# Two key/value heads per load on alternate partitions, in a decode kernel of two attention and two MLP layers

## The chip, the core and the metric

The kernel runs on one core of one Trainium2 chip. The metric is the device time of one execution in microseconds; the kernel before took 231.98 us, the median of three runs (231.31 to 232.46). A core has five engines with queues of their own: TensorE (PE in the profile, with PEld for its weight loads), VectorE (DVE), ScalarE (ACT), GpSimd (POOL) and SyncE (SP), which here issues nearly all DMAs. Each engine works through its own list in order and waits on semaphores for the others.

## The reference

Eight sequences, one new token each, width D = 448. One layer is attention over a cached window and then an MLP; the pair is applied twice with the same weights and the same cache:

```python
x = x + attention(layernorm(x), k_cache, v_cache, wq, wo)   # 16 query heads, 8 key/value heads, Dh 256
x = x + mlp(layernorm(x), w1, w2)                           # 448 -> 1792 -> 448, silu
x = x + attention(layernorm(x), k_cache, v_cache, wq, wo)
x = x + mlp(layernorm(x), w1, w2)
```

Only the last 1024 of the 4096 cached positions count. For each sequence and each of its 8 key/value heads that is 1024 x 256 bf16 of K and as much of V: 512 KB each, 128 such pieces, 67.1 MB in all, beside some 10 MB of weights. Two query heads share one key/value head. Each piece is needed in both layers and is loaded once.

## The kernel before

**Loads.** `load_kv` fetches one head of K or V (512 KB) into one of R = 30 buffers `slot`, by one DMA (L496): partition p holds positions 8p to 8p+7, a row of 4 KB. The order is K heads 0 to 7 of sequence 0, V heads 0 to 7, K of sequence 1, and so on (`seq`, `pump`). Load n waits until load n-30 has been used for the last time. `wq` (rows of 8 KB, contiguous) is loaded first, `w2` and `wo` behind K of sequence 0, `w1` behind V of sequence 0.

**One sequence b.** K is turned in place by VectorE in 32 x 32 blocks of 4 bytes (`transposes`, L639): four heads with one instruction of 128x1024, four with two of 128x512. `scores` (L656) multiplies the 16 query heads with K: 32 matmuls of 256 columns for each half of the heads (four heads side by side on four column groups of TensorE), read with a step of two elements. `softmax` takes the maximum (L673), spreads it over the partitions with a float32 matmul against `quad` (L675, L677), the exponential (L688), a reordering matmul against `perm` (L690, 256 columns) and a turn (L692) that gives the weights of the values. `products` (L703) multiplies them with V: four matmuls of 512 columns for each head, each writing rows that the next head overwrites from row 4(8-kvh) down. In layer 1 the last two heads (`late`, `products_late`, L712) go to an own bank, so that the other six heads can be evicted (L725), turned (L729, L733) and multiplied with `wo` (L754) before the last V has landed. `fold` and `xcols` (L760, L529, L532, L765) bring the residual row into columns; `chain` is the MLP (L544, L549, L798, L806, L818) and the query projection of layer 2 (L833, L838, L839, L846, L850). Then layer 2 scores, softmax and products on the same K and V follow, after which their slots are free.

**Order.** Layer 2 of sequence b is mixed with layer 1 of sequence b+1. The order of every engine is written out as lists of task numbers (`ORDER`); semaphores are derived from it. `warm` puts groups of four matmuls without use (L781) into TensorE's list.

**End.** The MLP of layer 2 is done for sequences 0 to 6 together (`final_rows`; its constants L874, L878, L880) and for sequence 7 alone (`final_last`: L798, L801, L803, L959, L963).

Of the kernel before, what the change touches and what calls it, by code (L numbers as in the profile page):

```python
# [14 lines left out]
        "196 69 74 86 87 88 89 197 198 92 136 94 199 137 138 139 148 149 161 150 200 151 201 154 202 203 157 204 205 "  # L15
        "159 206 207 208 209 228 229 211 213 225 226 231 227 233 235 214 237 215 240 216 242 217 218 248 249 219 275 "
        "276 251 257 220 254 259 264 262 325 277 279 280 278 281 282 221 312 222 313 267 314 315 287 288 223 318 289 "
        "321 290 224 326 327 328 329 323 330 331 343 297 344 333 300 340 341 351 342 346 335 352 353 302 348 354 355 "
        "350 356 357 371 374 376 336 358 409 382 383 368 410 411 385 388 393 391 398 396 412 413 414 415 416 446 447 "
        "448 449 401 337 338 421 452 422 423 424 459 455 339 431 460 461 462 463 434 457 464 465 484 476 477 467 436 "  # L20
        "469 473 474 479 475 481 485 486 483 487 504 509 507 488 489 490 491 515 516 501 542 543 518 521 524 526 531 "
        "529 544 470 546 547 548 549 545 534 579 554 580 581 582 555 556 557 471 585 564 472 588 592 567 593 594 595 "
        "596 590 617 618 597 598 569 609 619 610 600 606 607 612 608 620 621 614 616 602 637 640 642 622 623 675 624 "
        "676 648 649 634 603 604 651 654 657 659 664 662 677 725 679 680 681 682 678 712 713 667 714 715 687 688 689 "
        "718 605 690 721 697 726 727 728 729 730 723 731 742 700 733 743 750 751 752 753 735 739 740 745 741 754 702 "
        "747 755 749 756 757 770 773 775 808 736 767 781 782 809 810 784 787 792 790 797 795 812 813 814 815 811 800 "
        "845 846 847 848 820 821 737 822 851 738 823 854 830 856 859 860 861 833 862 875 863 864 883 876 866 858 884 "
        "885 886 872 887 878 873 874 880 888 882 835 889 903 890 906 908 868 900 941 914 915 942 917 869 920 925 923 "
        "930 928 943 944 945 946 947 948 978 979 980 981 933 870 984 871 953 954 987 955 956 992 993 994 995 989 996 "
        "997 1008 991 963 999 1001 1009 966 1005 1006 1011 1007 1013 1016 1017 1002 1015 968 1018 1036 1041 1039 "  # L30
        "1019 1020 1021 1022 1023 1047 1048 1033 1074 1075 1050 1076 1053 1056 1058 1063 1061 1077 1078 1079 1066 "
        "1080 1081 1084 1085 1086 1087 1105 1106 1107 1108 1090 1111 1118 1093 1003 1004 1114 1142 1143 1144 1119 "
        "1116 1120 1121 1122 1123 1124 1145 1134 1146 1147 1126 1095 1135 1131 1132 1137 1133 1139 1148 1128 1149 "
        "1141 1129 1154 1157 1151 1159 1197 1198 1165 1166 1199 1200 1168 1130 1171 1176 1174 1181 1179 1196 1202 "
        "1250 1224 1184 1225 1226 1227 1237 1238 1239 1240 1211 1208 1233 1251 1246 1252 1253 1235 1254 1259 1248 "
        "1260 1261 1262 1256 1213 1264 1258 1266 1218 1268 1219 1271 1274 1284 1276 1221 1285 1286",
    "dve":
        "37 28 39 43 34 26 36 46 42 25 38 24 5 13 4 54 7 32 44 40 18 30 33 6 22 27 45 50 11 57 31 29 9 49 52 70 15 "
        "19 72 51 73 132 75 58 134 3 84 80 81 59 76 60 141 82 48 135 77 133 10 53 83 140 143 35 16 55 146 144 142 78 "
        "20 17 145 90 91 85 93 14 174 12 21 175 56 147 169 184 185 152 41 170 155 162 163 179 158 160 47 8 189 180 "  # L40
        "190 271 272 236 273 241 243 245 23 247 274 252 309 258 304 310 260 261 311 307 308 306 305 265 266 316 319 "
        "322 295 324 298 301 405 406 407 370 408 375 303 377 379 381 438 441 439 386 442 444 394 392 395 445 443 440 "
        "399 400 450 453 429 456 432 435 458 538 539 503 540 510 508 514 437 512 541 573 571 519 575 576 525 527 528 "
        "574 532 577 572 533 578 583 562 586 565 589 568 591 671 672 570 673 636 674 641 643 645 647 705 706 708 652 "
        "707 711 658 660 661 704 710 709 665 666 716 719 695 722 698 724 701 804 805 703 806 769 807 774 776 778 780 "
        "837 839 838 785 840 842 793 791 794 843 844 798 799 841 849 852 828 855 831 857 834 937 938 939 902 836 940 "
        "907 909 911 913 971 970 973 918 975 977 926 924 927 972 974 976 931 932 982 985 988 961 990 964 967 1070 "
        "1071 1035 1072 1042 1040 969 1046 1044 1073 1098 1100 1051 1099 1101 1057 1059 1060 1097 1064 1065 1103 "
        "1102 1104 1088 1109 1091 1112 1094 1115 1117 1096 1186 1153 1158 1188 1160 1189 1162 1187 1193 1164 1169 "
        "1190 1191 1177 1192 1194 1175 1195 1178 1182 1183 1204 1206 1228 1229 1207 1230 1231 1241 1242 1243 1244 "  # L50
        "1234 1247 1236 1209 1249 1212 1214 1215 1217 1269 1275 1277 1279 1280 1282 1283 1222 1287",
    "act":
        "2 71 164 165 166 167 171 172 176 153 177 168 178 181 182 156 183 186 187 191 188 192 210 212 230 193 232 "
        "234 238 95 173 244 246 250 253 255 263 268 317 320 296 332 299 334 345 347 349 372 378 380 367 384 369 387 "
        "389 397 402 451 454 430 433 466 468 478 480 482 505 513 511 500 517 520 502 522 530 535 584 563 587 566 599 "
        "611 601 613 615 638 644 646 633 650 635 653 655 663 668 717 720 696 699 732 744 734 746 748 771 766 777 779 "
        "783 786 788 768 796 801 850 853 829 832 865 877 867 879 881 904 899 910 912 916 901 919 921 929 934 983 986 "
        "962 998 965 1000 1010 1012 1014 1037 1045 1043 1032 1049 1034 1054 1052 1062 1067 1089 1110 1092 1113 1125 "
        "1127 1136 1138 1140 1150 1155 1152 1161 1163 1167 1201 1170 1172 1180 1203 1205 1185 1232 1245 1255 1263 "
        "1257 1265 1216 1267 1220 1272 1270 1278 1281",  # L60
    "pool":
        "0 1 79 130 131 239 269 270 256 404 403 373 390 536 506 523 537 669 639 656 670 802 772 789 803 905 935 936 "
        "922 1068 1069 1038 1055 1156 1173 1210 1273",
}

# [158 lines left out]
def bass_interleave_layers__sliding_block_cached__dense_activation_silu__decode_kernel(  # L224
# [15 lines left out]
    FC = F // P  # L240
    SCALE = float(DH) ** -0.5
    EPS = 1e-5
    R = 30
    WIDE = (0, 1, 2, 3)
    LATE = 2
    WARM = (8, 12, 5, 4, 4, 4, 4, 4, 3)
# [243 lines left out]
    def slot_key(s):  # L490
        return [("slot", s, 0), ("slot", s, 1)]
# [607 lines left out]
```

## Time and profile before

| | |
|---|---|
| median of three runs | 231.98 us (231.31 to 232.46) |
| the profiled execution's own time | 230.15 us |
| its span (first to last instruction) | 228.4 us |
| instructions | 8452, of which 3779 matmuls |
| busy: PE, PEld, DVE, ACT, POOL | 173.0, 94.1, 157.2, 71.4, 22.8 us |
| granted TensorE clock | 1.0 throughout |
| moved by DMA | 78.21 MB |

The page gives shares over the whole span. It also cuts the span into 40 slices of 5.7 us; a digit is the busy share in tenths. Groups of instructions are named by engine, line and the tiles that they write and read, with the count, the busy time together, the mean of one in nanoseconds, and what ended the idle time before them. The view by windows gives the same for any stretches one names; its last two columns are the busy share of the DMA engines and the GB/s that they moved. Where this text says when one load landed, it is the time of its issue plus its time from issue to landing in the trace. Matmul durations overlap, since matmuls are pipelined: the pace of a burst is its length divided by its count.

### The profile page before, as it was taken

To read this page: it belongs to the slowest core of one execution; us is meant where nothing else is said; L and a number is where in the kernel's file an instruction comes from. 1 tells how busy PE (TensorE), PEld (TensorE's weight loads), DVE (VectorE), ACT (ScalarE), POOL (GpSimd) and SP (SyncE) were. 2 spreads that over 40 slices of the span, in tenths; PEclk is the share of its full clock that TensorE was granted. 3 is DMA by queue.
4 is the path that set the end of the run, shared out by engine and by line. 5 is a ranking of instruction groups with operands and counts; after the bars stand their busy time and mean duration, and the time that the engine had idled before them with its cause. 6 is when DMAs were issued, how large, how long until landed. Compare 5 with 4: busy or idle time off the path is not lost.

```text
span 228.4 us, 8452 instructions
## 1 busy us (share of the span) xinstructions
PE 173.0 (76%) x3779; PEld 94.1 (41%) x3779; DVE 157.2 (69%) x369; ACT 71.4 (31%) x218; POOL 22.8 (10%) x41
## 2 busy tenths in 40 slices
PE   0020737357878989999898987888989999999894
PEld 0010623123444455445444644554445445544662
DVE  6238989878792797389459837974895589314644
ACT  2000080633302341432324142414332431353341
POOL 1000130000200210101010101110120200000020
PEclk9999999999999999999999999999999999999999
DMA  6999999999999999999999999999999999700000
GB/s 175 413 406 407 382 380 395 411 414 417 405 400 369 377 408 403 396 408 407 406 406 408 402 378 411 408 392 395 410 409 385 380 408 406 307 3 3 0 6 1
DMA packets 22681, 78.21 MB, mean 342 GB/s; under 512 B 2279, under 2 KB 5302, under 8 KB 22262
## 3 DMA queue, kind: packets, MB, share of 16 engines
q1 hardware_dynamic: 22486, 77.32, 86.6%
q8 instruction: 29, 0.48, 0.9%
q10 hardware_dynamic: 160, 0.36, 0.6%
q14 instruction: 6, 0.05, 0.1%
HBM read 77.67 MB, written 0.01 MB: 340 GB/s over the span
## 4 chain that ended last, share of the span: by engine, by line
PE 46%; DVE 31%; DMA 10%; ACT 6%; issue 4%; SPq 2%; DVEq 0%; ACTq 0%
DVE slot L639 12%; DMA slot<-in_A_k_cache_dram 10%; PE bank L656 10%; PE bank L703 7%; DVE slot L472 7%; PE pair L754 6%; PE bank L781 2%; PE pair L833 2%; ACT ot L760 2%; PE bank L675 2%; PE bank L846 2%; PE bank L712 2%; PE bank L833 2%; PE pair L529 2%; PE pair L818 1%
## 5 line engine op out<-in xcount | busy, mean ns | idle before, releaser
L639 DVE STREAM_TRANSPOSE slot<-slot 128x512 uint32<-128x512 uint32 (+1 forms) x96 | 80.2, 866 | 7.0 <-DMA slot<-in_A_k_cache_dram 6.8
L656 PE MATMUL bank<-slot,qbd 128*16 128x256 bf16 (+1 forms) x1024 | 40.9, 285 | 5.1 <-DVE slot L639 2.0
L703 PE MATMUL bank<-slot,qbd 128*24 128x512 bf16 (+6 forms) x416 | 31.1, 393 | 3.5 <-DVE qbd L692 3.3
L656 PEld LDWEIGHTS bank<-slot,qbd 128*16 128x16 bf16 (+1 forms) x1024 | 23.2, 87 | 16.7 <-ACT qbd L850 4.0
L781 PE MATMUL bank<-wq_sb,cols 128*1 128x512 bf16 x192 | 19.6, 416 | 13.9 <-DMA wq_sb<-in_A_wq_dram 13.9
L776 POOL TENSOR_TENSOR fcols<-fcols 128x1 f32<-128x1 f32 x17 | 9.4, 554 | 106.4 <-ACT fcols L774 94.5
L754 PE MATMUL pair<-wo_sb,q1s 128*1 128x449 bf16 x288 | 17.2, 353 | 1.1 <-DVE wo_sb L475 0.8
L850 ACT ACTIVATE qbd<-bank 128x256 bf16<-128x256 f32 x16 | 6.1, 384 | 33.5 <-PE bank L846 33.5
L725 ACT ACTIVATE ot<-bank,q1s 128x512 bf16<-128x512 f32 (+1 forms) x16 | 10.8, 673 | 16.4 <-PE bank L703 11.1
L626 POOL TENSOR_TENSOR qbd<-q1s,fcols 128x256 bf16<-128x256 bf16 x16 | 9.7, 614 | 59.7 <-PE bank L712 42.4
L703 PEld LDWEIGHTS bank<-slot,qbd 128*24 128x24 bf16 (+6 forms) x416 | 9.7, 92 | 11.1 <-DVE qbd L692 4.2
L692 DVE STREAM_TRANSPOSE qbd<-bank 128x256 bf16<-128x256 bf16 x17 | 8.0, 473 | 8.2 <-PE bank L690 7.9
L673 DVE TENSOR_REDUCE q1s<-bank 128x1 f32<-128x256 f32 x15 | 6.3, 423 | 8.1 <-PE bank L656 8.0
L472 DVE TENSOR_REDUCE slot<-wo_sb 128x6 f32<-128x2688 bf16 x4 | 11.8, 2948 | 0.1
L781 PEld LDWEIGHTS bank<-wq_sb,cols 128*1 128x1 bf16 x192 | 4.2, 82 | 15.4 <-issue 13.9
L674 ACT ACTIVATE q1s<-fcols,q1s 128x4 f32<-128x4 f32 x15 | 4.4, 296 | 18.7 <-DVE q1s L673 18.7
L675 PE MATMUL bank<-q1s,quad 128*128 128x4 f32 x30 | 6.0, 269 | 4.7 <-ACT q1s L674 4.5
L598 PE MATMUL pair<-slot,wq_sb 128*128 128x16 bf16 x128 | 3.6, 174 | 7.5 <-DVE slot L591 7.5
L833 PE MATMUL pair<-wq_sb,q1s 128*1 128x256 bf16 x256 | 8.9, 275 | 0.3 <-DVE q1s L765 0.3
L688 ACT ACTIVATE qbd<-bank,q1s 128x256 bf16<-128x256 f32 x15 | 7.1, 472 | 6.3 <-DVE q1s L677 6.0
L712 PE MATMUL bank<-slot,qbd 128*7 128x256 bf16 (+7 forms) x192 | 8.6, 283 | 0.6 <-DVE qbd L692 0.6
L833 PE MATMUL bank<-wq_sb,q1s 128*1 128x512 bf16 x128 | 8.8, 390 | 0.0
(168 smaller groups left out, 244.6 us busy)
## 6 DMA issues: line engine op xcount, KB each, us to landing
slot<-in_A_k_cache_dram SPq DMA_DIRECT2D x64, 512.0 KB, 8.3
slot<-in_A_v_cache_dram SPq DMA_DIRECT2D x64, 512.0 KB, 10.1
wo_sb<-in_A_wo_dram SPq DMA_DIRECT2D x4, 896.0 KB, 14.6
wq_sb<-in_A_wq_dram SPq DMA_DIRECT2D x3, 1024.0 KB, 8.0
w_sb<-in_B_w_dram SPq DMA_DIRECT2D x1, 1568.0 KB, 19.8
w_sb<-in_B_w_dram SPq DMA_DIRECT2D x1, 1344.0 KB, 17.2
wq_sb<-in_A_wq_dram ACTq DMA_DIRECT2D x1, 256.0 KB, 3.5
wq_sb<-in_A_wq_dram SPq DMA_DIRECT2D x1, 256.0 KB, 4.1
```

Source lines behind the costliest of these rows:

```text
L472: dve(lambda e, rows=rows, s=s: e.tensor_reduce(s, rows[:, :, R0:M1].rearrange("p c (a n) -> p c a n", a=2), AX.X, ALU.add, negate=True), ...
L626: pool(lambda e, k2=k2: e.tensor_tensor(qdata(0, k2), q1s[:, b, 64 * k2:64 * k2 + 64].rearrange("p (n r) -> p n r", r=2).unsqueeze(3) .bro ...
L639: dve(lambda e, v=v: e.transpose(v, v), keys, keys, 0.15 + n / 2 / 950, b, ("KW%d" if n > 1024 else "KT%d") % k)
L656: fns.append(lambda e, w=w, j=j, kv=kv, cb=cb, par=par: e.matmul(sc[32 * j:32 * j + up_to, 0:256], w, kv, start=(cb == 0 and par == 0), st ...
L675: pe(lambda e: e.matmul(mx, quad[:], mq, start=True, stop=True, skip_group_check=True), [K[4], "quad"], bk(LB[n]), 0.2, b, "mx%d" % L)
L703: pe([lambda e, t=t: e.matmul(bank[ob][32 * t:32 * t + m, :], pT_sb[L][:, 64 * t:64 * t + m], v[:, 512 * t:512 * t + 512], start=True, sto ...
L712: pe([lambda e, t=t, a=a: e.matmul(o[32 * t:32 * t + m, :], pT_sb[n][:, 64 * t + a:64 * t + a + m], v[:, 512 * t + DH * a:512 * t + DH * a ...
L725: act(lambda e: e.activation(o_t, src[1], ACTF.Copy, scale=sm[b][:, 4 * L + 3:4 * L + 4]), bk(src[0]) + [("sm", b, L, 3)], okey, 0.62, b, ...
L754: fns.append(lambda e, i=i, w=w, c0=c0: e.matmul(bank[XB][32 * (i % 4):32 * (i % 4) + 1, c0:c0 + D + 1], oT[:, oT_col(i):oT_col(i) + 1], w ...
L776: pool(lambda e: e.tensor_tensor(rhalf, var4, nhalf, ALU.pow), ["var4", "nhalf"], ["rhalf"], 0.54, b, "pow" + name)
L781: pe([lambda e, i=i: e.matmul(bank[OB[0]][32 * i:32 * i + 1, :], zero_b, wq_sb[:, 512 * i:512 * i + 512], start=True, stop=True, tile_posi ...
L833: pe([lambda e, j=j, c=c, qh=qh, k2=k2, h=h, n=n: e.matmul(qh[32 * j:32 * j + 1, :], xbt[b][:, xcol(c, k2):xcol(c, k2) + 1], view(wq_sb[:] ...
```

## The change

- One DMA loads two heads (1 MB) into a slot of 8 KB per partition; there are 15 slots. Partition 2i holds positions 16i to 16i+15 of the first head, partition 2i+1 those of the second. The two heads lie 2 MiB apart in memory. The very last load is split into two of 512 KB with rows of 4 KB.
- `transposes` does the same number and sizes of instructions. Behind the turn the two heads alternate, so `scores` reads with a step of four elements instead of two.
- `softmax`: the maximum is spread by four small float32 matmuls on column groups instead of one of 128 partitions; the reordering is four matmuls of 128 columns that write every second column, instead of one of 256.
- `products` runs per pair, in two halves (8 of the 16 positions each) that accumulate; weights that belong to the other head are zeros. The count of matmuls is the same. `late` is the last pair.
- A slot is free when both its heads are done.
- The last MLP loses one VectorE step in each half (L801); the factor moves into the last instruction, which adds the residual that ScalarE has copied out earlier. Ten small VectorE instructions of `final_rows` move to an earlier sequence (`fold_consts`).
- All lists in `ORDER` are new.

```diff
-    R = 30
-    WIDE = (0, 1, 2, 3)
+    R = 15
+    NP = HKV // 2
+    WIDE = (0, 1)
+    SLOT = 4096
...
-        dma(lambda e: e.dma_start(slots[s][:, :].rearrange("p (u d) -> p u d", d=DH),
-                                  cache[b, kvh, S0:SK, :].rearrange("(p u) d -> p u d", p=P)),
-            slot_key(s) + extra, W * DH * 2, "slot%d" % s)
+        a = cache[b, 2 * j, S0:SK, :]
+        step = SLOT // 2 if apart else SLOT
+        for h in range(SLOT // step):
+            src = bass.AP(a.tensor, a.offset + h * step, [[SLOT, 64], [SK * DH, 2], [1, step]])
...
-                    kv = slots[slot_of[b, "k", 4 * k2 + j]][:, :].rearrange(
-                        "p (u cb jj par) -> p cb par u jj", u=8, cb=4, par=2)[:, cb, par, :, :]
+                    kv = view(slots[slot_of[b, "k", 2 * k2 + j // 2]][:, :], 64 * cb + 2 * (j % 2) + par, [(256, 16), (4, 16)])
...
-            pe(lambda e: e.matmul(mx, quad[:], mq, start=True, stop=True, skip_group_check=True), [K[4], "quad"],
-               bk(LB[n]), 0.2, b, "mx%d" % L)
+            pe([lambda e, t=t: e.matmul(mx[32 * t:32 * t + 32, :], quad[:], mq[:, 4 * t:4 * t + 4], start=True, stop=True,
+                                        tile_position=(0, 32 * t), skip_group_check=True) for t in range(4)],
+               ["mq", "quad"], bk(LB[n]), 0.06, b, "mx%d" % L)
...
-        pe(lambda e: e.matmul(px, perm[:], e_sb[m], start=True, stop=True),
+        pe([lambda e, h=h, u=u: e.matmul(px[:, h:256:2], perm[h][:, 16 - 16 * u:144 - 16 * u],
+                                         e_sb[m][:, 128 * u:128 * u + 128], start=(u == 0), stop=(u == 1),
+                                         skip_group_check=True) for h in range(2) for u in range(2)],
...
-        m = 4 * (HKV - kvh)
-        pe([lambda e, t=t: e.matmul(bank[ob][32 * t:32 * t + m, :], pT_sb[L][:, 64 * t:64 * t + m],
-                                    v[:, 512 * t:512 * t + 512], start=True, stop=True, tile_position=(0, 32 * t),
-                                    skip_group_check=True) for t in range(4)],
+        m = 8 * (NP - j)
+        for h in range(2):
+            pe([lambda e, t=t, h=h: e.matmul(
+                bank[ob][32 * t:32 * t + m, :], pT_sb[L][:, 64 * t + 32 * h:64 * t + 32 * h + m],
+                v[:, 2048 * h + 512 * t:2048 * h + 512 * t + 512], start=(h == 0), stop=(h == 1),
+                tile_position=(0, 32 * t), skip_group_check=True) for t in range(4)],
...
-                dve(lambda e, t=t: e.tensor_scalar(t, t, 1.0, rhalf, op0=ALU.add, op1=ALU.mult), [("th", h), "rhalf"],
-                    [("th", h)], 0.12, b, "th" + n)
...
-        dve(lambda e: e.tensor_copy(orow, ob[:, 0:T]), bk(OB[1]) + KEY, ["orowL"], 0.18, b, "orowL")
+        dve(lambda e: e.scalar_tensor_tensor(out=orow, in0=ob[:, 0:T], scalar=rhalf, in1=res, op0=ALU.mult, op1=ALU.add),
+            bk(OB[1]) + ["rhalf", "resL"] + KEY, ["orowL"], 0.2, b, "orowL")
...
-    cap = [R - 2]
+    cap = [R - 1]
```

The new lists move these places, by the order of the instructions (counted before and after): in the last batch TensorE's list has the turn of the first six heads (L729, 12 columns) ahead of the last late products (L712, 3 rows) before, and behind all 16 late products and four other products after. VectorE's list has, at the start, three row sums of `wo` and two of `w2` ahead of the first turn of softmax (L692) before, and two and one after. At the end VectorE's copy of the seven other rows (L927) stands behind both products of the last MLP (L803) before, and between its two halves after.

## The prediction

> **What bounds the kernel now.** I read the page's slices first, to see which resource is full and until when; then windows, for the rate of loads with rows of 8 KB and of 4 KB; then, sequence by sequence, when V landed and when TensorE used it, to see which of the two waits; last the tail.
>
> ```profile
> DMA  6999999999999999999999999999999999700000
> GB/s 175 413 406 407 382 380 395 411 414 417 405 400 369 377 408 403 396 408 407 406 406 408 402 378 411 408 392 395 410 409 385 380 408 406 307 3 3 0 6 1
> ```
>
> The DMA engines are full from slice 2 to 35, until about 199 us; the remaining 29 us are a chain of small steps. So the time is the stream's length plus a tail, as long as compute keeps up with the stream.
>
> ```profile
> 8.00:12.00 4.00, 0.00 (x0) 0.00 (x0) 0.00 (x0) 0.00 (x0) 0.00 (x0) 1.00 1.01 422
> 28.00:36.00 8.00, 4.07 (x76) 1.95 (x68) 7.01 (x13) 4.69 (x14) 2.44 (x3) 1.00 1.06 381
> ...
> 60.00:64.00 4.00, 3.41 (x81) 1.76 (x79) 2.89 (x7) 1.00 (x3) 0.55 (x1) 1.00 1.03 410
> ...
> 192.00:196.00 4.00, 3.43 (x91) 2.51 (x88) 2.74 (x7) 1.15 (x4) 0.00 (x0) 1.00 1.03 411
> ```
>
> The last column of the windows is GB/s. From 8 to 12 us only `wq` moves, in rows of 8 KB: 422. From 28 to 36 us it is `w2` and `wo` in rows of 1792 B: 381. In windows of K and V alone, in rows of 4 KB, it is 410 to 412 (mean of five: 411).
>
> Now the compute. The last V head of sequences 1 to 7 landed at 73.16, 95.02, 116.00, 137.14, 157.64, 178.70 and 200.36 us; TensorE began its late products of that head (L712, 3 rows) at 74.48, 95.42, 116.45, 137.54, 158.68, 179.44 and 200.68.
>
> ```profile
> 200.41 0.26 PE L729 MATMUL bank<-sel_o,ot 128*128 128x12 bf16 x4
> 200.59 0.24 PE L694 MATMUL bank<-q1s,lsel 128*32 128x1 f32 x8
> 200.68 0.40 PE L712 MATMUL bank<-slot,qbd 128*3 128x256 bf16 x8
> 200.94 0.93 PE L754 MATMUL pair<-wo_sb,q1s 128*1 128x449 bf16 x16
> ```
>
> So compute follows the stream by 0.3 to 1.3 us. Stream and compute are balanced: a shorter stream pays only as far as the new order makes compute shorter too. TensorE is busy 17.8 of each 20 us from 80 to 180 us (mean of five windows), which at 21.03 us a sequence (126.20 us from 74.48 to 200.68, by six) is 18.7, with 2.3 us left, some of it filled with L781, which nobody needs.
>
> **The change part by part.**
>
> *Loads.* K and V are 67.1 MB: 163.3 us at 411 GB/s, 159.0 at 422, so **-4.3 us**. From the extremes (412 to 421, the second from 6 to 12 us) it is -3.5. No row of the trace shows a load that alternates between two regions 2 MiB apart; as a loss that is a rival below. I take -4.0. The dips in the GB/s row (369, 378, 380) are stalls that rows of 8 KB meet as well. At the end two loads of 512 KB with 4 KB rows cost nothing beyond before.
>
> *Freeing slots.* Load n+30 heads waits for the same score or product groups as before, two heads at a time, so at most one head's 1.28 us later. Before, the tightest issues (66.93, 72.30, 151.62, 172.60 us) landed 4.7 to 4.8 us later with the queue still full ahead of them; the last two landings are 1.25 us apart, so it never ran dry. Cost 0, and up to +1.0 if an issue comes 1.28 us later in the first two sequences, where the margin is smallest.
>
> *K by pairs.* The first head of a pair is there 1.28 us later. VectorE waits for K 6.8 us in all (9 times), only on the first heads; the last transposition of sequence 7 began at 193.16, 3.6 us after the last K landed (189.55), because it stood behind L838. So the later heads don't notice: 0, at most +1.0 where VectorE has no gap left.
>
> *Scores with a step of four.* The count and shape stay. L656 with a step of two elements runs 80 in 2.60 us, 32.5 ns each for 256 columns; L703, contiguous, 24 in 1.48 us, 61.7 ns for 512. So a step of 4 bytes costs 5% at most. A far step does cost: L884 reads 42 columns 256 bytes apart in 237 ns, L532 42 columns side by side in 182, 1.3 ns a column. The bounds for a step of 8 bytes are therefore 0 and 1.3 ns a column; nearest is L656's own 4 bytes, so I take 0. The Trainium skill (SBUF — State Buffer, "Door 1: The DMA port swizzle") says that SBUF has lines of 16 bytes, of which two accesses in a row are needed for full speed. By it a step of 8 bytes is just free and L884's is not, with which the rows agree; by it the sum stays as it is.
>
> *Reordering in softmax.* One matmul of 256 columns (283 ns) becomes four of 128 that write every second float32. Contiguous, from L738 (6 columns, 179 ns) and L690 (256, 283 ns) the slope is 0.42 ns a column, so four take about 0.23 + 3 x 0.056 = 0.40 us. L846 writes every fourth column, 64 columns at a pace of 66 ns (four begin at 64.63, 64.70, 64.76, 64.82), some 1 ns a column: four of 128 would then take 0.7. So +0.1 to +0.4 per softmax. The four small matmuls for the maximum replace L675 (0.39 us for its two passes) and resemble L694 (x8 in 0.24): -0.15. In the steady part this is spread among TensorE's gaps; in the tail only the reordering counts. I take **+0.2**.
>
> *Products.* 32 groups of the same size, nothing.
>
> *Start.* Two of the row sums before the first turn (2.95 and 1.99 us) now stand behind it. `wo` could begin at 53.34 when its sums were done (idle <- DVE L475); with one sum of `w2` less ahead it is ready about 2 us earlier, and then V's landing at 48.7 rules: products 2.1, L725 0.7, L729 0.3, L733 0.2 put it at about 52.1. This 1.2 us only lets compute catch up with the stream: 0 in the sum.
>
> *Last batch.* The turn of six heads now stands behind the late products. Before, `wo` began 0.58 us after the last landing and its 32 rows were done after 2.5 us. Now it is landing +0.3, products until +1.0 (the groups follow at 0.2 us), turn, L733 0.2, so `wo` from +1.25, done at +3.15: **+0.6**.
>
> *End.* L801 goes from both halves (0.21 and its gap: 0.26), but the copy of the seven rows (L927, 605 ns) now stands between the halves, and the second half is late by about what the first gains; of the ten constants only two memsets lay near the path. 0, within 0.2 either way.
>
> Sum: -4.0 + 0.2 + 0.6 = **-3.2 us** on the profiled execution's 230.15, which is 226.95. That execution was 1.83 us below the median of the three runs; I forecast the median: 231.98 - 3.2 = **228.8 us**. A measurement of this kernel can tell about 0.5% (1.16 us) from no change. The forecast's own range is 227.6 to 230.2: from -4.3 with no loss in the last batch to -1.8 with one of the +1.0 terms; chance 0.52.
>
> **The rivals.**
>
> *The compute keeps its pace (0.17).* The late products of the last but one head (L712, 7 rows) went from 73.85 to 199.63, 20.96 us a sequence, while the stream allowed 21.24 (71.66 to 199.10), and lagged where the stream was quick: from 137.54 to 158.68 it took 21.14 us though V came after 20.50. For it: that lag, and TensorE at 89%. Against it: sequences 4 and 6 took 20.3 us between those products (116.02 to 136.30, 157.82 to 178.06), so 20.5 is within reach. Then only the start's 1.2 us is won, the order at the end costs nothing, softmax 0.2: 231.0 us.
>
> *More is won (0.17).* The whole 4.3 is passed on, TensorE comes to the turn early enough that the last batch loses nothing, the end gains 0.2 and softmax costs its lower 0.1: 231.98 - 4.4 = 227.6 us, down to 226.4 with a start that also shortens the stream's first waits.
>
> *Slower: scores pay for the step (0.08).* The place is L656's 128 matmuls per sequence. It decides from 2.3 us / 128 = 18 ns a matmul on, TensorE's idle time. At twice the pace (+32.5 ns) it is 4.2 us a sequence, 1.9 beyond the idle time in seven sequences, and 64 matmuls in the tail, 2.1: +15 us, 247; at 1.3 ns a column far more. Against it: L656 against L703.
>
> *Slower: two regions 2 MiB apart load slower than one (0.06).* As slow as the slowest stream seen, 381 GB/s, it is 176.1 us for K and V, +12.8: 245 us; it decides from 411 GB/s down. For it there is no row, against it only that `wq` at 422 shows what 8 KB rows can do in one region. The Trainium skill (DMA: Bandwidth & Descriptors, "Latency and other measured facts") gives 164 GB/s for rows 2 MiB apart against 207 at 512 KiB or 214 with padding. By that ratio, 0.77, K and V would take 212 us and the kernel 281; but there every row was 2 MiB from the last, here neighbours are 8 KB apart within each head, so it speaks for the direction alone.
>
> **How the numbers follow.** 0.52 for the forecast, 0.17 and 0.17 for the milder rivals, 0.14 for slower. Faster by over 0.5% (below 230.8): 0.52 + 0.17 + 0.06 of the compute case = 0.75; within 0.5%: the remaining 0.11 of it; slower: 0.14. The range 226.6 to 231.9 leaves out the 0.14 and some 0.05 at the low end.
>
> **What would show it.** K and V windows at 418 to 422 GB/s instead of 411, with the last load landing at 196 to 197.5 us; L656's burst still at 31 to 34 ns a matmul; the four reordering matmuls in 0.4 to 0.7 us; `wo` of sequence 0 near 52; the last `wo` done about 3 us after the last landing; the tail after that as long as before. I am wrong if the GB/s don't rise, if scores go over 50 ns, or if the lag between V's landing and its products grows sequence by sequence to 2 us or more (then compute is the bound).

## The result and the profile after

The changed kernel takes **255.52 us** (median of four runs, 254.58 to 256.25), the kernel before 231.88 beside it: ratio 1.102, 95% interval 1.096 to 1.107. The forecast was 228.8. The profiled execution has a span of 254.2 us. Here and below a time is the median of all executions of a kernel; some executions take 1.5% or more longer than the shortest, and the ratios, each to the kernel before run beside it, leave these out. The median before moved between 230.98 and 231.98 us from one series to the next, so small differences are read from the ratios.

The page of the kernel after, the rows of the DMA engines and of what they moved:

```profile
DMA  6999999999799919995999699679976996400000
GB/s 176 416 416 405 380 392 422 417 427 419 295 410 404 420 80 373 427 416 199 423 424 384 235 433 397 277 298 344 391 297 219 427 423 265 164 3 5 0 3 4
```

Where before the row was full from slice 2 to 35, the engines now run dry once in every sequence (slices 11, 15, 19, 23, then 26 and 27, 30 and 31, 34), and between the holes they are faster than before. The windows of the kernel after say the same (last columns: the granted clock, which is the share of full speed that TensorE's throttle allowed, the DMA share, GB/s):

```profile
40.00:44.00 4.00, 0.25 (x8) 0.16 (x8) 3.85 (x9) 2.81 (x10) 0.00 (x0) 1.00 1.01 416
60.00:64.00 4.00, 3.22 (x77) 1.70 (x73) 3.90 (x7) 1.07 (x3) 0.37 (x1) 1.00 1.01 420
84.00:88.00 4.00, 4.00 (x90) 2.09 (x88) 3.75 (x9) 2.21 (x6) 0.55 (x1) 1.00 1.01 422
92.00:96.00 4.00, 4.00 (x72) 2.07 (x68) 2.09 (x4) 0.38 (x1) 0.00 (x0) 1.00 0.14 29
```

Rows of 8 KB give 416 to 422 GB/s instead of 411, two regions 2 MiB apart or not. In the last window TensorE is busy all the time and the loads stand still: they wait for slots. What TensorE does is seen in its timeline, one burst of scores before and one after (start, length, count at the end):

```profile
192.43 2.60 PE L656 MATMUL bank<-slot,qbd 128*16 128x256 bf16 x80
```
```profile
190.74 4.38 PE L669 MATMUL bank<-slot,qbd 128*16 128x256 bf16 x72
```

That is 32.5 ns a matmul before and 60.8 after. The groups of both kernels (busy time, mean of one, idle time before and its cause; L656 and L690 are before) have the scores at 408 ns each instead of 285, and the reordering at 10.8 us instead of 4.9. The reordering now reads twice the columns, since each of its 256 results is summed from two matmuls:

```profile
L656 PE MATMUL bank<-slot,qbd 128*16 128x256 bf16 (+1 forms) x1024 | 40.9, 285 | 5.1 <-DVE slot L639 2.0
L690 PE MATMUL bank<-qbd,perm 128*128 128x256 bf16 x17 | 4.9, 289 | 3.1 <-ACT qbd L688 2.9
L669 PE MATMUL bank<-slot,qbd 128*16 128x256 bf16 (+1 forms) x1024 | 66.3, 408 | 8.0 <-DVE slot L653 3.4
L703 PE MATMUL bank<-qbd,perms 128*128 128x128 bf16 x68 | 10.8, 316 | 4.3 <-ACT qbd L701 4.2
```

The timeline of the last batch, which answers the one shown of before:

```profile
223.46 0.62 PE L730 MATMUL bank<-slot,qbd 128*7 128x256 bf16 x16
...
224.23 0.26 PE L747 MATMUL bank<-sel_o,ot 128*128 128x12 bf16 x4
...
224.91 1.70 PE L772 MATMUL pair<-wo_sb,q1s 128*1 128x449 bf16 x32
```

The last V had landed at 221.40, so TensorE came to it 2.1 us late, where it was 0.3 before.

A table made from the traces shows where the time came in: when the first `wo` matmul of layer 1 began in sequences 0, 1 and 7, the mean from 1 to 7, and what is left after the last. The runs e1 to e18 follow below.

| | seq 0 | seq 1 | seq 7 | a sequence | rest |
|---|---|---|---|---|---|
| before | 53.34 | 75.62 | 200.94 | 20.89 | 27.4 |
| after | 53.70 | 80.68 | 224.91 | 24.04 | 29.3 |
| e2, before with a step of four | 53.44 | 77.58 | 218.94 | 23.56 | 29.1 |
| e1, after with a step of two | 52.78 | 76.64 | 204.85 | 21.37 | 27.6 |
| e6, K in rows of 4 KB | 52.94 | 76.81 | 205.27 | 21.41 | 27.5 |
| e18, e1 with slots free early | 52.28 | 76.07 | 201.84 | 20.96 | 27.6 |

Of the 25.8 us between the spans, 0.4 are at the start, 4.7 in the first sequence, 18.9 in the six that follow (3.15 each) and 1.9 in the tail.

### The profile page after: what moved, and what is told of

Its sections match the earlier page's. It is cut to its first block, busy times and chain, and to the rows that moved or that the text cites. A ratio compares the mean times of both kernels' runs of the same rounds, so it can differ in the third digit from the quotient of the medians.

```text
span 254.2 us, 8680 instructions
## 1 busy us (share of the span) xinstructions
PE 198.9 (78%) x3920; PEld 106.2 (42%) x3920; DVE 155.8 (61%) x369; ACT 71.3 (28%) x219; POOL 22.8 (9%) x41
## 4 chain that ended last, share of the span: by engine, by line
PE 65%; DVE 16%; ACT 7%; DMA 7%; issue 2%; SPq 2%; DVEq 0%; ACTq 0%
PE bank L669 22%; PE bank L719 9%; DVE slot L653 7%; DMA slot<-in_A_k_cache_dram 7%; PE pair L772 6%; PE bank L703 4%; PE bank L799 4%; PE pair L845 2%; PE bank L858 2%; DVE slot L480 2%; PE pair L830 2%; ACT ot L743 2%; PE bank L845 2%; PE bank L747 2%; PE pair L542 2%
## 5 line engine op out<-in xcount | busy, mean ns | idle before, releaser
L653 DVE STREAM_TRANSPOSE slot<-slot 128x512 uint32<-128x512 uint32 (+1 forms) x96 | 79.7, 865 | 11.8 <-DMA slot<-in_A_k_cache_dram 11.7
L669 PE MATMUL bank<-slot,qbd 128*16 128x256 bf16 (+1 forms) x1024 | 66.3, 408 | 8.0 <-DVE slot L653 3.4
L669 PEld LDWEIGHTS bank<-slot,qbd 128*16 128x16 bf16 (+1 forms) x1024 | 30.2, 101 | 31.5 <-DVE slot L653 7.1
L719 PE MATMUL bank<-slot,qbd 128*24 128x512 bf16 (+3 forms) x416 | 30.1, 383 | 0.0
L743 ACT ACTIVATE ot<-bank,q1s 128x512 bf16<-128x512 f32 (+1 forms) x16 | 10.8, 673 | 25.9 <-PE bank L719 19.4
L686 ACT ACTIVATE fcols<-fcols,q1s 128x16 f32<-128x16 f32 x15 | 4.7, 310 | 38.7 <-DVE q1s L685 37.1
L862 ACT ACTIVATE qbd<-bank 128x256 bf16<-128x256 f32 x16 | 6.1, 384 | 29.1 <-PE bank L858 29.1
L703 PE MATMUL bank<-qbd,perms 128*128 128x128 bf16 x68 | 10.8, 316 | 4.3 <-ACT qbd L701 4.2
L719 PEld LDWEIGHTS bank<-slot,qbd 128*24 128x24 bf16 (+3 forms) x416 | 9.9, 93 | 8.7 <-issue 2.2
L783 DVE TENSOR_TENSOR q1s<-pair,fcols 128x5 bf16<-128x5 f32 x17 | 2.8, 166 | 13.2 <-PE pair L545 13.1
L712 DVE RECIPROCAL q1s<-bank 128x1 f32<-128x1 f32 x17 | 2.5, 160 | 13.1 <-PE bank L709 13.0
L488 ACT ACTIVATE slot<-w_sb 128x448 bf16<-128x448 bf16 x6 | 3.5, 577 | 24.4 <-DMA w_sb<-in_B_w_dram 24.2
L703 PEld LDWEIGHTS bank<-qbd,perms 128*128 128x128 bf16 x68 | 5.9, 121 | 8.2 <-ACT qbd L701 7.6
```

The source lines that it names most:

```text
L653: dve(lambda e, v=v, i0=i0, i1=i1: e.transpose(v, v), keys, keys, 0.15 + (i1 - i0) * 512 / 950, b, ("KW%d" if i1 - i0 > 1 else "KT%d") % ( ...
L669: fns.append(lambda e, w=w, j=j, kv=kv, cb=cb, par=par: e.matmul(sc[32 * j:32 * j + up_to, 0:256], w, kv, start=(cb == 0 and par == 0), st ...
L703: pe([lambda e, h=h, u=u: e.matmul(px[:, h:256:2], perm[h][:, 16 - 16 * u:144 - 16 * u], e_sb[m][:, 128 * u:128 * u + 128], start=(u == 0) ...
L719: pe([lambda e, t=t, h=h: e.matmul(bank[ob][32 * t:32 * t + m, :], pT_sb[L][:, 64 * t + 32 * h:64 * t + 32 * h + m], v[:, 2048 * h + 512 * ...
L743: act(lambda e: e.activation(o_t, src[1], ACTF.Copy, scale=sm[b][:, 4 * L + 3:4 * L + 4]), bk(src[0]) + [("sm", b, L, 3)], okey, 0.62, b, ...
```

## The experiments

**e1, e2: the step alone, taken out of one kernel and put into the other.**

```diff
 e1 (after)   - 64 * cb + 2 * (j % 2) + par, [(256, 16), (4, 16)]
              + 64 * cb + 32 * (j % 2) + par, [(256, 16), (2, 16)]
 e2 (before)  - "p (u cb jj par) -> p cb par u jj"
              + 64 * cb + par, [(112, 16), (4, 16)]
```

> The kernel after with one number changed: the scores read K with a step of two elements (4 bytes) instead of four, the same count of columns from the same slots, so that the columns belong to other positions and heads than they should; everything else stays. Theory (the step alone is the cause): the burst of 72 score matmuls falls from 60.8 ns a matmul to 32 to 33 ns, that is 128 x 28.3 = 3.6 us less in each of seven sequences and 64 x 28.3 = 1.8 us less in the tail, 27 us in all: 228.5 us, between 226.5 and 231. Rival A (the new orders and the pairs are the cause, the step only shows beside them): the matmuls get faster as well, but the loads still wait for slots, and the time stays above 240. Rival B (compute keeps the pace of before): 231 to 232.

> The kernel before with the scores reading K with a step of four elements instead of two inside the same slots, 256 columns as before; the columns belong to other positions and other parts of the head than they should; loads, orders and softmax as before. Theory (the step alone): 60 to 61 ns a matmul instead of 32.5, and most of the added 3.6 us a sequence passes through: 7 x 2.5 to 3.6 + 2 for the tail: 250 to 259 us. Rival A (the new orders and pairs turn it into time): the pace is the same, but only what goes beyond TensorE's idle time of 2.3 us a sequence counts, 7 x 1.3 + 2: 243 us. Rival C (the slow pace belongs to the paired layout): the pace stays at 32.5 ns and the time at 232.

e1: 234.68 us, ratio to before 1.011 (1.006 to 1.016). e2: 249.89, ratio 1.077 (1.071 to 1.082). A burst of scores in e1, then one in e2:

```profile
65.82 2.09 PE L669 MATMUL bank<-slot,qbd 128*16 128x256 bf16 x64
```
```profile
208.27 4.74 PE L655 MATMUL bank<-slot,qbd 128*16 128x256 bf16 x80
```

In e2 80 matmuls take 4.74 us, 59.3 ns each; in e1 64 take 2.09 us, 32.7. So the step costs 20.8 us in the new kernel and 17.9 in the old one, without pairs, new orders or other loads. In the table, 2.67 us a sequence come with it in both, of 3.6 and 3.4 us of added matmul time (128 times 28.3 and 26.8 ns): three quarters pass through. But e1 does not reach the forecast: it is slower than before, and rival B's 231 to 232 is missed too.

The page of e1 shows that its loads still run dry, less and later:

```profile
DMA  6999999999999996999899999999997998500000
GB/s 175 419 422 413 376 380 413 418 422 423 420 375 417 420 417 259 423 422 410 310 423 417 375 419 422 420 334 398 423 413 293 422 422 345 189 3 3 0 6 1
```

**e4, e8: what a step costs.** e4 is the kernel after with `(3, 16)` for `(4, 16)`. e8 replaces twelve groups of matmuls without use by bursts; only the pace of these counts, not its 288.38 us (one run).

> The kernel after with the scores reading with a step of three elements (6 bytes), other columns than they should. If TensorE's read pays for the bytes that its step spans, shared among the four matmuls that run side by side, with nothing to pay up to 4 bytes: 60.8 x 6/8 = 46 ns a matmul. If it pays for leaving every second element as one threshold (anything over 4 bytes is twice as slow): 61 ns. If only steps of 8 bytes and more are slow: 32 to 33 ns. Each ns is 0.13 us a sequence: at 46 ns about 241 us.

> The kernel after, with the last twelve groups of matmuls without use of sequence 0 replaced by twelve bursts of 24 matmuls of 256 columns; only their pace counts, not the kernel's time. Seven bursts run on four column groups in turn, each with a region of its own, with steps of 1, 2, 3, 4, 6, 8 and 16 elements; three on a single column group with steps of 2, 4 and 8; one on four column groups that all read the same columns with a step of 4; one over all 128 rows and columns with a step of 4. Theory A (four matmuls side by side share one stream of 16-byte lines; a single matmul does not use it up): 29, 29, 45, 57, 85, 113 and 113 ns; on one column group about 120 ns each with steps of 2, 4 and 8, which is four times 29; the same columns: 57; all rows: about 120. Theory B (each matmul pays for its own step, alone or not): the single column group doubles from a step of 2 to a step of 4, to 230 ns. Theory C (a threshold between 4 and 6 bytes): steps of 6, 8 and 16 elements stay near 57 ns.

e4 took 247.14 us (one run). Its burst of 72 takes 3.69 us, 51.3 ns a matmul, between 32.5 and 60.8: above the 46 of the one expectation and below the 61 of the other:

```profile
183.78 3.69 PE L669 MATMUL bank<-slot,qbd 128*16 128x256 bf16 x72
```

The timeline of e8, one line a burst of 24 matmuls: four column groups with steps of 1, 2, 3, 4 and 8 elements, then a single column group with 4 and 8, then the same columns for all four with 4:

```profile
53.52 0.83 PE L805 MATMUL bank<-wq_sb,cols 128*1 128x256 bf16 x24
54.17 0.85 PE L806 MATMUL bank<-wq_sb,cols 128*1 128x256 bf16 x24
55.47 1.25 PE L807 MATMUL bank<-wq_sb,cols 128*1 128x256 bf16 x24
56.89 1.59 PE L808 MATMUL bank<-wq_sb,cols 128*1 128x256 bf16 x24
...
61.53 2.94 PE L810 MATMUL bank<-wq_sb,cols 128*1 128x256 bf16 x24
...
71.34 5.60 PE L813 MATMUL bank<-wq_sb,cols 128*1 128x256 bf16 x24
79.57 10.98 PE L814 MATMUL bank<-wq_sb,cols 128*1 128x256 bf16 x24
98.27 1.59 PE L815 MATMUL bank<-wq_sb,cols 128*1 128x256 bf16 x24
```

Steps of 6 and 16 took 2.55 and 2.98 us; the single group with a step of 2 took 2.92, all 128 rows with a step of 4 took 5.66. By the time between starts, a matmul on one column group takes 113, 226 and 450 ns with steps of 2, 4 and 8; four side by side take the same each and so a quarter of it in pace. Theory A's count of lines fits the curve (full up to four elements from 16 bytes, then time in proportion to the lines, no dearer from 8 elements on), but its sharing falls: each matmul pays for its own step, alone or not, as theory B has it. Theory C falls.

**e3, e6, e9, e12: can the scores keep a step of two?** e3 lets the transposition write the two heads apart. e6 loads K in rows of 4 KB, one head behind the other, and the exponential puts the columns into order. e9 and e12 let the loads put the heads on blocks of 16 or of 4 partitions, with four loads a pair.

```diff
 e3   + o = view(slot half as u32, 0, [(32, 16 * (i1 - i0)), (1, 16), (16, 2)]);  e.transpose(o, v)
 e6   + src (K) = [[SLOT // 2, P], [SK * DH, 2], [1, SLOT // 2]]
      + scores: 2048 * (j % 2) + 64 * cb + par, [(256, 8), (2, 32)]
      + exp reads view(bank[sb], 0, [(1, 2), (32, 8), (2, 16)])
 e9   + slots[s][32 * g:32 * g + 32] <- [[SK * DH, 2], [SLOT, 16], [1, step]]        g = 0..3
 e12  + slots[s][i:P:4] <- [[4 * SLOT, 16], [SK * DH, 2], [1, step]]                 i = 0..3
```

> The kernel after with the transposition of K writing the columns of the first head into the first 64 bytes of each block of 32 x 4 bytes and those of the second head into the other 64 bytes; the scores then read with a step of two elements. Theory: VectorE's 96 transpositions keep their mean of 865 ns (the same bytes, written in another order), the scores come to 32.5 ns, and the time is that of the run with a step of two, 228.5 us. Rival: the permuted write costs VectorE; at a mean of 1.3 us or more its 156 us of busy time grow by 42 or more, VectorE becomes the bound, and the time is 245 or more. Between them: each 100 ns on the mean is 1.2 us a sequence, which VectorE (61% busy) can hide in part.

> The whole computation, with pairs, products, softmax and orders of the kernel after, but K loaded in rows of 4 KB (two heads one behind the other in each partition), so that the scores read with a step of two elements; the exponential reads its 256 columns in another order (three dimensions, 8 bytes apart) and writes them in that of the kernel after. Theory (the chain of 21.5 us is the bound): 234.7 plus what the exponential loses, 0 to 0.2 us a sequence: 234.5 to 236.5; faster than the kernel after by 20 us, still slower than before. Rival (the stream is the bound): half of 4.3 us more than the run with a step of two, 236.8 and more. Rival (a far read in the exponential is dear): its mean over 0.9 us instead of 0.6, 238 or more.

> The whole computation. The kernel after, with the two heads of a pair on partitions 32g to 32g+15 and 32g+16 to 32g+31 instead of even and odd ones: four loads of 32 partitions (256 KB, rows of 8 KB) take the place of one of 1 MB, the scores read 16 columns with a step of two elements for each head, and the reordering matmuls write runs of 16 float32 instead of every second one. Theory (the step is one cause, the chain of 21.5 us a sequence the other): scores at 29 ns a matmul as in the run with a step of two; the reordering 0.61 us or down to 0.4, twice a sequence in the chain; loads at 420 GB/s: 232.5 to 235. Rival (small loads are slower, or SyncE's 256 issues of 0.4 us hold the stream up): windows of K and V under 410 GB/s and 236 or more.

> The whole computation. As the run with blocks of 16 partitions, but with the heads of a pair changing every four partitions, and each of the four loads of a pair taking every fourth partition: its outermost dimension has 16 steps, where that of the blocks had two (only two of 16 DMA engines worked there, 53 GB/s). Scores read runs of four columns with a step of two elements, which fill 16 bytes; the reordering matmuls write runs of four float32. Theory: the DMA engines share the rows by the outermost dimension, so windows of K and V are back at 415 to 422 GB/s; scores at 29 to 33 ns a matmul; the rest is the chain: 232.5 to 235.5. Rival (256 issues of 0.43 to 0.6 us each on SyncE, four times as many, hold the stream up): 237 or more.

e3: 262.39 us, ratio 1.131 (1.126 to 1.136). Its group of transpositions:

```profile
L655 DVE STREAM_TRANSPOSE slot<-slot 128x512 uint32<-128x512 uint32 (+1 forms) x96 | 120.5, 1339 | 10.7 <-DMA slot<-in_A_k_cache_dram 10.5
```

1339 ns instead of 865, so the rival was right: VectorE is busy with them for 120.5 us instead of 79.7, 40.8 more, where TensorE is busy with the scores for 41.0 instead of 66.3, 25.3 less. e6: 234.94 us, ratio 1.013 (1.005 to 1.020), as expected by the chain; it is the fastest run here that does the whole computation with the change, 20 us faster than the kernel after and still behind the one before. e9: 1341.65 us, ratio 5.79 (5.77 to 5.82); the page:

```profile
DMA  4152121111111111111111111111111111111110
GB/s 150 53 146 90 53 86 53 53 53 53 53 53 53 53 53 53 53 54 53 53 53 53 53 53 53 53 53 54 53 53 53 53 53 53 53 53 53 53 51 4
```

53 GB/s is an eighth of 420, and the DMA share is 0.13 (from 300 to 400 us): a load whose outermost dimension has two steps kept two of 16 engines busy. The Trainium skill (DMA: Bandwidth & Descriptors, "Why a DMA increments its semaphore by 16 and not by 1") says that the count of engines comes from the slowest dimension of the two sides, and the trace agrees. e12, with 16 steps outermost, took 292.83 to 310.94 us (median 300.68); its ratio, from the two shortest of six, is 1.266 (1.260 to 1.272). In its profiled execution (302.53 us) the DMA engines are full (share 9 in nearly every slice) and move 282 GB/s from 100 to 200 us. The rival's time (237 or more) came, but not by its cause: the DMA engines have no holes in which they wait for SyncE's issues, so the loads themselves are slow. Why rows that go to every fourth partition are, stays open.

**e5, e7, e11: is the stream the bound?** e5 is e1 with the loads in rows of 4 KB. e7 drops the matmuls without use in sequences 1 to 7 of the kernel before; e11 gives it the four small matmuls for the maximum.

```diff
 e5   + src = [[SLOT // 2, P], [SK * DH, 2], [1, SLOT // 2]]          (all but the last pair)
 e7   - for i in range(4)        + for i in range(4 * (b == 0))       (warm)
 e11  - mx = quad[128x128] x mq  + four of 128 x 32, tile_position=(0, 32 * t)
```

> The run with a step of two, and its loads (all but the last pair of V) in rows of 4 KB as before instead of 8 KB, two heads a load as in the kernel after; the heads do not alternate on the partitions any more, so that positions and weights belong to other values than they should. It asks whether the faster stream is worth anything. In the run with a step of two, one sequence takes 21.5 us from the end of the scores of layer 2 to the same point of the next one, all of it steps of TensorE, VectorE and ScalarE that follow each other, and the late products start 1.8 us after V has landed. Theory (this chain is the bound, not the stream): the windows of K and V alone fall from 420 to 411 GB/s and the time stays at 234.7, within 1 us. Rival (the stream is the bound): the 67.1 MB take 4.3 us longer, and the time goes to 238 to 239.

> The kernel before without the groups of four matmuls that nobody needs (L781) in sequences 1 to 7, three to five groups a sequence; all that is needed stays. They cost about 0.22 us each where TensorE does not wait: about 0.9 us a sequence. Theory (in the kernel before, too, the chain of 20.9 us a sequence is the bound and the stream only just keeps up): what lies in the chain goes, some 0.3 to 0.6 us a sequence, until the stream bounds: 228 to 230.5. Rival (the stream alone bounds the kernel before): 231.5 to 232.5. Rival (TensorE's granted clock falls when it is less busy): slower than 232, with a clock under 1.0.

> The kernel before with one part of the change alone: the maximum is spread by four small float32 matmuls on column groups instead of one against 128 x 128. Theory: 0.39 us become 0.24, once a sequence in the chain, about 1 us in all at most; the stream holds part of it back: 231 to 232, that is, at the limit of what can be told from no change. Rival: it costs as much or more, 232 to 233.

e5: 235.95 us, ratio 1.014 (1.005 to 1.023): 1.3 us over e1 in the medians, 0.8 by the ratios, with overlapping intervals, not 4.3. So the faster stream is worth little there. e7: 231.26, ratio 0.998 (0.993 to 1.002), and e11: 231.87, ratio 1.000 (0.996 to 1.004): no change that can be told. The profiled execution of e7 had a mean granted clock of 0.97, with dips in slices 8 to 10; but other executions of e7 had 1.00 and some of the kernel before 0.978, so the runs do not show that the edit lowers it.

**e10, e13, e14, e15, e16: shorter chains of instructions.** In e10, e13 and e14 (on e9, e12 and e6) TensorE's list loses one to three groups without use and one product ahead of the late products; e15 (on e6) moves one instruction of VectorE; e16 does both.

```diff
 e10, e13, e14  PE:  ... perm, [fill], perm, [fill], PV1, PV0 x6, [PV1], PV7, ...   [x] moved away
 e15            DVE: - KW0 KW1 KW2 xb1 KW3      + KW0 KW1 xb1 KW2 KW3       (sequences 1, 2, 5, 6)
```

> The run with blocks of 16 partitions, and TensorE's list changed: of the groups of matmuls without use, those between the last scores and the late products of a sequence (one to three) go to places after the products of the MLP and of the query projection, where TensorE waits; a product of layer 2 that stood before the late products goes behind them (three sequences). Same work, same loads. Theory (the chain bounds): 0.2 to 0.5 us a sequence less, 1 to 3 us in all: 230.5 to 233. Rival (the stream, or the slots, bound the run with blocks): no change within 0.7 us.

> The run with blocks of four partitions, and TensorE's list changed as in the trimmed run before: of the groups of matmuls without use, those between the last scores and the late products of a sequence (one to three) go to places after the products of the MLP and of the query projection, and a product of layer 2 goes from before the late products to behind them (three sequences). Same work, same loads. Theory (the chain bounds): 0.2 to 0.5 us a sequence less, 1 to 3 us in all. Rival (the stream or the slots bound it): no change within 0.7 us.

> The run with K in rows of 4 KB and V in rows of 8 KB (234.9), with TensorE's list changed in the same way. Theory (the chain bounds): 1 to 3 us less, 232 to 234. Rival (stream or slots): 234.2 to 235.6.

> The run with K in rows of 4 KB and V in rows of 8 KB (234.9), with one place in VectorE's list changed, in four of the sequences (1, 2, 5 and 6): the instruction that brings the residual into columns ahead of the MLP (128x5) stands before the third transposition of the next K instead of behind it. That transposition waits for the second pair of K to land, and TensorE's first matmul of the MLP waits for the columns: 2.4 us in sequence 1 and 1.8 in sequence 5 instead of 0.8. Theory (a loop over one sequence decides there: end of the scores of layer 2, slot free, load, landing of K, VectorE, MLP, query projection, scores of layer 2): some 1.0 to 1.25 us less in sequences 1 and 5 and as much at most in 6: 231.5 to 233.5. Rival (what is won is given back at the next wait, as it was with the trimmed list): 234.3 to 235.3.

> Both changes of order in one kernel: TensorE's trimmed list and VectorE's moved instruction, on the run with K in rows of 4 KB. Theory: the 0.27 us a sequence that the trimmed list won between reordering and late products was given back at VectorE's wait for K; with that wait shorter it stays: 1 to 2 us less than e15, 230.5 to 232.5. Rival: as e15, within 0.5 us.

e10 (1342.76, ratio 5.80, 5.78 to 5.83) and e13 (300.19, ratio 1.297, 1.291 to 1.302) tell nothing of the order, since their loads set the time. e14: 235.01, ratio 1.017 (1.013 to 1.021); e15: 237.15, ratio 1.026 (1.021 to 1.030); e16: 236.16, ratio 1.021 (1.017 to 1.026). The theory fell each time; e16 came 1.0 us below e15, as its theory said, but with overlapping intervals and far above 230.5 to 232.5. e14 did shorten its stage (first reordering to late products 3.30 us instead of 3.57, mean of five sequences), and the period stayed (21.58 against 21.56, from one release of a K slot to the next). In e15 (means of sequences 2 to 6) the MLP began 0.83 us after the fold instead of 1.35, but from there to the query projection it took 0.67 us more, so the projection came 0.15 us later behind the fold. VectorE's timeline in e15 shows why:

```profile
98.72 1.25 DVE L655 STREAM_TRANSPOSE slot<-slot 128x1024 uint32<-128x1024 uint32 x1 [2.93 <-DMA slot<-in_A_k_cache_dram]
...
101.08 0.12 DVE L787 TENSOR_TENSOR q1s<-pair,fcols 128x5 bf16<-128x5 f32 x1
101.28 2.37 DVE L655 STREAM_TRANSPOSE slot<-slot 128x1024 uint32<-128x1024 uint32 x2
103.58 0.42 DVE L564 STREAM_TRANSPOSE pair<-pair 128x256 f32<-128x256 f32 x1
```

The columns (L787) come earlier, but the MLP's next step (L564) then stands behind two transpositions of K, and all of them began late because K landed late (2.93 us idle until the load).

**e17, e18: the loads need not wait for the scores of layer 2.** On e6 and on e1:

```diff
+        ks = 1 if layer else k2
-        slots[slot_of[b, "k", 2 * k2 + j // 2]]
+        slots[slot_of[b, "k", 2 * ks + j // 2]]
```

> The run with K in rows of 4 KB and V in rows of 8 KB (234.9), in which layer 2 takes the scores of heads 0 to 3 from the slots of heads 4 to 7, so that it computes these from the wrong keys: the same matmuls, but the slots of the first two pairs of K are free after layer 1, some 20 us earlier, and the last pair of V and the first K of the next sequence need not wait for the scores of layer 2. Nothing else changes. Theory L (a loop through the slots holds the rest: end of the scores of layer 2, slot free, load, landing of K, VectorE, MLP, query projection, scores of layer 2): the 7.9 us of gaps between landings mostly go and the time falls to 230 to 232.5. Rival C (the chain of TensorE, VectorE and ScalarE is as long without the loads): 234 to 235.5, with the queue of the DMA full.

> The same change on the run with a step of two elements (234.7), which loads K and V in rows of 8 KB at 420 GB/s and besides reads other columns than it should. Theory L: 228 to 231, the time that was forecast for the change, and 0.5 to 2 us below e17, since the faster stream now counts. Rival C: 234 to 235.

e17: 232.45 us, ratio 1.005 (1.002 to 1.007); e18: 232.40, ratio 1.004 (1.001 to 1.008). Both fell, by 2.5 and 2.3 us in the medians and by 1.9 and 1.5 us by the ratios (whose intervals still overlap), so the wait for slots held 60% or more of what e6 and e1 lost to before. But the two are alike, though one loads K at 411 and the other at 420 GB/s (their last loads land 0.6 us apart, at 197.75 and 197.17 us), and e18 does not get to 228 to 231: theory L is right for this part and wrong for the rest. The page of e18, and its last batch in TensorE's timeline:

```profile
DMA  6999999999999999999999999999999999000000
GB/s 176 414 424 410 380 381 412 416 423 421 419 421 414 421 413 421 416 419 414 421 404 414 419 390 367 424 393 380 383 383 390 409 416 385 34 3 3 0 6 1
```
```profile
198.53 1.34 PE L720 MATMUL bank<-slot,qbd 128*32 128x512 bf16 x20
...
200.39 0.62 PE L731 MATMUL bank<-slot,qbd 128*7 128x256 bf16 x16
...
201.84 1.69 PE L773 MATMUL pair<-wo_sb,q1s 128*1 128x449 bf16 x32
```

This is the stream that was forecast: full to slice 34, the last load landed at 197.17 us, 3.2 us ahead of before. Yet the late products began 3.2 us after it, and `wo` at 201.84, 0.9 later than before. From 55 us on VectorE waits only 1.4 us for K, and TensorE's list of waits has no load of V in it. So in e18 the engines' own steps take the 20.96 us a sequence, where one took 20.89 before.

## Why the prediction was wrong, point by point

**Scores with a step of four: the step that failed.** It was taken as 0 between bounds of 0 and 1.3 ns a column, after the nearest row, L656 with 4 bytes. Measured: 60.8 ns a matmul instead of 32.5, 0.44 ns a column more for each (226 against 113 ns for 256 columns), inside the bounds and far from the end that was chosen. The other end was no outlier either: steps of 8 elements and more cost 1.3 ns a column in e8 (450 against 113 ns), as L884's did. A row that shows 4 bytes to be free says nothing of 8: four elements of a 16-byte line are what full speed needs, and two give half of it. The Trainium skill (SBUF — State Buffer, "Door 1: The DMA port swizzle"), by which two accesses in a line are enough, speaks for the value I took; e8 shows otherwise for TensorE's moving reads. The worth is 20.8 us by e1 against the kernel after.

**The rival "scores pay for the step" (0.08, 247 us)** had the mechanism, the place and the price (twice the pace). It was short by 8.5 us. It took TensorE's idle time as cover and let 1.9 of 4.2 us a sequence pass, where 2.67 of 3.6 did: 5.4 us in seven sequences. Another 2.7 us are what the rest of the change lost (e1 against before), which was no part of it. Idle time inside a chain of steps that wait for each other covered 0.9 of 3.6 us here.

**Loads, -4.0.** The rate is right (416 to 422 GB/s), and in e18 the last load landed at 197.17 as forecast (196 to 197.5). It was worth nothing: with the last load 3.2 us ahead of before, the last `wo` of e18 began 0.9 us later. The view that misled is the one of V's landing and TensorE's late products: a lag of 0.3 to 1.3 us was read as "compute follows the stream". It only showed that the two were tied. Here the rival "the compute keeps its pace" (0.17) is right: without slow scores and without waiting for slots the time is 232.4, near its 231.0, and a sequence takes 20.96 us. Single sequences of 20.3 us, which spoke against it, did not show a pace that all of them could keep.

**Freeing slots, 0 and up to +1.0; K by pairs, the same.** Too small: 2.3 to 2.5 us together by the medians of e17 and e18, 1.5 to 1.9 by the ratios. Load 23 (the last V of sequence 2) waits in e1 until 88.91 us for the scores of layer 2 of sequence 1, when the DMA had less than one load left (the one before landed at 90.05). The first K behind it landed at 97.63, and VectorE idled until then; in e18 the two came at 79.06 and 94.16. From 55 us on VectorE waits 9.3 us for K in e1, 5.6 before and 1.4 in e18.

**Reordering** takes 0.61 us instead of 0.28, +0.33, within the 0.1 to 0.4. **The maximum** takes 0.25 instead of 0.39, as forecast; alone it is worth nothing (e11). **Products** cost the same.

**Start:** `wo` of sequence 0 at 52.28 to 52.94 where scores are fast (52.1 forecast), and 53.70 in the kernel after. What was won is lost again on the way to sequence 1: 23.8 us in e18, 22.3 before. Which of the new orders does it isn't settled. **Last batch, +0.6:** not seen, since TensorE comes after the landing anyway. **End:** 27.6 against 27.4 us in e18, within the 0.2; the kernel after loses 1.9, which is what its 64 slow scores add (64 x 28.3 ns = 1.8 us). **Two regions 2 MiB apart** cost nothing (416 to 422 GB/s).

So the sum is: 255.5 with the step (ratio 1.102), 234.7 without (1.011), 232.4 without the wait for slots as well (1.004), 231.9 before. Why the last 0.4% are lost stays open. No run here beat the kernel before beyond the noise; the closest, e7, has a ratio of 0.998 (0.993 to 1.002).

## What to carry to other kernels

A cost that the trace does not show is not near the row that is nearest in kind: when the bounds are far apart and the operation runs a thousand times, measure it in one small run before anything is built on it. A small lag between a stream and its consumer says that they are tied, not which one leads; to see that, make the stream slower or free its buffers early, as e5 and e18 do. Where several loops are nearly as long as each other (slots, VectorE's list, the chain of a sequence), a stage made shorter comes back as a wait at the next one.

## What the runs showed of the hardware that was not expected

- TensorE's moving read of bf16 runs at full speed with steps of 1 and 2 elements (113 ns for 256 columns on one column group), at half with 4 (226), at a quarter with 8 (450) and no slower with 16; four column groups side by side pay alike, on the same columns or not. In the burst with a step of 8 the granted clock fell from 1.00 to 0.50 at 84 us, and the matmuls stayed 451 ns apart: the far read, not TensorE's clock, sets that pace.
- Early in the run, after idle stretches, 32 scores took 1.88 us in e1 and 2.04 in the kernel after (granted clock 1.00 in both), 58.8 and 63.8 ns a matmul: where TensorE was slow anyway, the step cost 5 ns instead of 28.
- A transposition of 32 x 32 blocks that writes its 4-byte columns 64 bytes apart takes 1339 ns instead of 865 (e3).
- Loads whose outermost dimension has two steps move 53 GB/s (e9); loads of 32 rows to every fourth partition move 282 with all engines busy (e12).
